# Cross-covariance attention and a squared-ReLU MLP on one core: a later second product for the first group, spread-out weight preparation, and another order of the last matmuls and stores

## Chip, cores and metric

The kernel runs on 1 core of one Trainium2 chip. The metric is the device time in microseconds of one execution, lower is better. The granted clock of the core's TensorE is given beside it where it matters.

## What is computed

```python
def _attn_ref(q, k, v, tau):                  # q, k, v: [4, 6080, 256] float32
    qn = q / (np.linalg.norm(q, axis=1, keepdims=True) + 1e-06)
    kn = k / (np.linalg.norm(k, axis=1, keepdims=True) + 1e-06)
    s = kn.transpose(0, 2, 1) @ qn / tau      # [4, 256, 256]
    s = s - s.max(-1, keepdims=True)
    a = np.exp(s)
    a /= a.sum(-1, keepdims=True) + 1e-09
    return (v @ a).astype(np.float32)
...
def _moe_ref(x, w_in, w_out, s, b):           # x: [24320, 256], w_in: [256, 2048], w_out: [2048, 256]
    h = x @ w_in
    r = np.maximum(h, 0.0)
    g = s * (r * r) + b
    return (g @ w_out).astype(np.float32)
```

The attention's output, reshaped to 24,320 rows, is the input `x` of the second function.

## The kernel before

For each of the 4 batches a 256 x 256 Gram matrix of k and q is summed over 6,080 rows, with the squares of k and q beside it. From it come the attention weights, and these are multiplied into `w_in` ("folds", lines 264 to 292), so that the MLP's first product is v times a folded 256 x 2048 weight `wa`.

**The start.** Batch 0 is done ahead of everything else: its rows come in 13 chunks (0 to 12), the last two with half as many rows per partition. For each chunk TensorE does the Gram matmuls (`mm`, line 142), and ScalarE and VectorE the squares. After some of the chunks the loop at line 398 calls `keep_busy` (line 392), matmuls whose result nobody reads. Then `finish_ops` computes the softmax and the first folds; six further folds are put into the main loop by `at_step`.

**The main loop.** The 24,320 rows of v are cut into groups of 512 rows (48 groups, 0 to 47; the last has 256). One step `s` of the loop at line 685 is one of the 16 tiles of 128 hidden features of one group, `g, m = divmod(s, 16)`. At each step the program emits, in this order:

- `mm1` (line 532): two matmuls from the transposed v and `wa` into half of an `h_ps` PSUM tile; there are two such tiles, each for two steps. The same two are used by the transposes of v by TensorE for groups 0 and 1.
- for group g - 1 some of the 112 matmuls of `seven_items` (line 670), which do the product with `w_out` in seven products instead of eight, with the sums `S1` to `S4` of g and with the weight combinations `T1`, `T2`, `T3`, `N4`. They start at tile `SHIFT` = 3 of group g.
- for the groups in `plain` (0 and 47), `plain_mm2` (line 578): the plain product with `w_out`, four matmuls a step for a whole group and two for the last group. It is `PLAG` = 5 steps behind `mm1`.
- on odd steps `relu` (line 542, ScalarE) of two steps' `h_ps`; then squares (lines 553 and 555), sums (lines 598 to 604), and what `at_step` has put on this step.

What `at_step` puts on steps includes `rowconst_sum` (lines 424 and 427, VectorE: the sum of the rows of `w_out`, in pieces `w`), `rowconst_mm` (line 431 on TensorE, line 432 on VectorE; every evacuation adds its result `rowconst`), and `combine_w` (lines 440 to 446), which makes T1, T2, T3 and N4 out of the four pieces: per piece and half-step two VectorE operations and one ScalarE copy that reads the result of one of them. `load_v`, `crossbar_v` (transposing DMAs on SP's queue), and the Gram work of the later batches are placed in the same way; Gram work of batch 1 starts at step 26. The PSUM tile of `rowconst_mm` is the one that the Gram sum of the next batch and the folds use.

`po` keeps the program's order on every engine, DMA queues included: a waiting instruction holds up all that come behind it on its engine. `store` (line 565) sends a finished group from `o_sb` to HBM on SP's queue.

Of the kernel before, what the change touches and what calls it, by code (L numbers as in the profile page):

```python
# [16 lines left out]
def kernel(  # L17
# [12 lines left out]
    nc = tc.nc  # L30
    P = 128
# [14 lines left out]
    FT = Dff // P  # L46
    TG = 512
    NG = (NT + TG - 1) // TG
# [5 lines left out]
    def po(ins):  # L54

        tc.keep_in_program_order(ins)
        return ins
# [296 lines left out]
    g0 = grams[0]  # L354
# [27 lines left out]
    NPIECE = FT // 4  # L382
# [6 lines left out]
    g0.start()  # L389
    NCH0 = len(g0.chunks)  # L390

    def keep_busy(n, w, x):

        idle_ps = h_tile("idle_ps")[:, 0, :]
        for _ in range(n):
            po(nc.tensor.matmul(idle_ps, w, x, start=True, stop=True, skip_group_check=True))

    for c in range(NCH0):
        ops = g0.norm_ops(c)
        if c >= NCH0 - 3:  # L400
            g0.add_norms()
        for j in range(g0.chunks[c][2]):
            g0.mm(c, j)
        if NCH0 - 4 <= c < NCH0 - 1:
            keep_busy(3, g0.tiles[c][1][:, 0, :P],
                      g0.tiles[c][0][:, :2, :].rearrange("p j c -> p (j c)"))
        for f in ops:
            f()
# [13 lines left out]
    def rowconst_sum(i):  # L422
        if i < NPIECE - 1:
            po(nc.vector.tensor_add(acc, w_pieces[0] if i == 0 else acc, w_pieces[i + 1]))
        else:
            n = 2 if i == NPIECE - 1 else 1
            po(nc.vector.tensor_add(acc[:, :n], acc[:, :n], acc[:, n : 2 * n]))
# [6 lines left out]
    def combine_w(i, step):  # L434
        w = w_pieces[i].rearrange("p (i h) c -> p h i c", h=2)
        B11, B12 = w[:, 0, :, :P], w[:, 0, :, P:]
        B21, B22 = w[:, 1, :, :P], w[:, 1, :, P:]
        part = ts(i, 2)
        if step == 0:
            po(nc.vector.tensor_sub(T1[:, part, :], B12, B11))  # L440
            po(nc.vector.tensor_sub(B12, B22, B12))
            po(nc.scalar.copy(out=T3[:, part, :], in_=B12))
        else:
            po(nc.vector.tensor_add(B12, B12, B11))
            po(nc.scalar.copy(out=T2[:, part, :], in_=B12))
            po(nc.vector.tensor_sub(N4[:, part, :], B21, B12))
# [4 lines left out]
    def at_step(s, f):  # L451
        side.setdefault(int(s), []).append(f)

    first_group = [b * N // TG for b in range(B)]
    for i, f in enumerate(fin[7:]):
        at_step(i // 2 * 4 + i % 2 + 1, f)
    at_step(14, lambda: po(nc.vector.tensor_scalar_mul(
        out=s_out, in0=s_bc, scalar1=1.0 / (LAM * LAM))))
    for i in range(NPIECE + 1):
        at_step(11 + i, lambda i=i: rowconst_sum(i))  # L460
    at_step(11 + NPIECE + 1, rowconst_mm)
    for i in range(NPIECE):
        for step in range(2):
            at_step(20 + i + 4 * step, lambda i=i, step=step: combine_w(i, step))
    for g in range(NG):
        if g >= 3:
            at_step(max(g - 4, 0) * FT + 2, lambda g=g: load_v(g))
# [89 lines left out]
    def evacuate(dst, src, add, n):  # L557
        if n == 1:
            add = add[:, None, :].broadcast_to((P, 2, add.shape[-1]))
        po(nc.vector.scalar_tensor_tensor(out=dst, in0=src, scalar=s_out, op0=ALU.mult,  # L560
                                          in1=add, op1=ALU.add))

    def store(g):
        t0, nj = group(g)
        po(nc.sync.dma_start(
            out=out[t0 : t0 + nj * P, :].rearrange("(p j) d -> p j d", j=nj),
            in_=o_sbs.pop(g)[:, :nj, :]))

    def plain_mm2(g, m):

        _, nj = group(g)
        for h in range((nj + 1) // 2):
            js = [j for j in (2 * h, 2 * h + 1) if j < nj]
            if m == 0:
                o_plain[g, h] = ps_o.tile([P, 2, C], FP32, tag="o_ps", name="o_ps")
            o = o_plain[g, h]
            for j in js:
                po(nc.tensor.matmul(  # L578
                    o[:, j % 2, :], g_tiles[g][:, m % 2, m // 2, ts(j, P)],
                    w_out16[:, m, :], start=(m == 0 and j == js[0]),  # L580
                    stop=(m == FT - 1 and j == js[-1]), skip_group_check=True))
            if m == FT - 1:
                if h == 0:
                    o_sbs[g] = opool.tile([P, TG // P, C], FP32, tag="o_sb", name="o_sb")
                evacuate(o_sbs[g][:, js[0] : js[-1] + 1, :], o, rowconst, 1)
                if js[-1] == nj - 1:
                    store(g)
# [18 lines left out]
    def seven_items(g):  # L606
        st = {}
        lo, hi = slice(0, P), slice(P, C)
        G = lambda h, t: lambda: g_tiles[g][:, h, :, ts(t, TG // 2)]
        W = w_out16.rearrange("p (i h) c -> p h i c", h=2)  # L610
        U = lambda: upool.tile([P, 2, P], FP32, tag="u", name="u")

        def out_sb(t, half):
            if g not in o_sbs:
                o_sbs[g] = opool.tile([P, TG // P, C], FP32, tag="o_sb", name="o_sb")
            return o_sbs[g][:, ts(t, 2), half]

        def p1():
            st["u1"] = U()
            evacuate(st["u1"], st["X"], rowconst[:, lo], 1)  # L620

        def p5():
            st["u5"] = U()
            evacuate(st["u5"], st["Z"], rowconst[:, hi], 1)

        def p6():
            st["u2"] = U()
            evacuate(st["u2"], st["X"], rowconst[:, hi], 1)

        def p2():  # L630
            evacuate(out_sb(0, lo), st["Y"], st["u1"], 2)

        def p7():
            evacuate(out_sb(1, hi), st["X"], st["u5"], 2)

        def p3():
            evacuate(out_sb(0, hi), st["Z"], st["u2"], 2)

        def p4():
            evacuate(out_sb(1, lo), st["X"], rowconst[:, lo], 1)  # L640
            store(g)

        def begin(name):
            t = ps_o.tile([P, 2, 2 * P], FP32, tag="o_ps", name="o_ps")
            halves = [t[:, h, :].rearrange("p (j c) -> p j c", j=2) for h in range(2)]
            if name == "X":
                st["X"] = halves[0]
                x_tile[0] = t
            else:
                st["Z"], st["Y"] = halves  # L650

        products = [
            ("X", G(0, 0), W[:, 0, :, lo], p1),
            ("Z", lambda: S[1], T1, p5),
            ("X", lambda: S[2], T2, p6),
            ("Y", G(1, 0), W[:, 1, :, lo], p2),
            ("X", lambda: S[3], T3, p7),
            ("Z", lambda: S[4], W[:, 1, :, hi], p3),
            ("X", G(1, 1), N4, p4),
        ]  # L660
        items = []
        for n, (name, a, w, after) in enumerate(products):
            for i in range(NP):
                for j in range(2):
                    def f(n=n, name=name, a=a, w=w, after=after, i=i, j=j):
                        first = n < 2 and i == 0 and j == 0
                        if first:
                            begin(name)
                        last = i == NP - 1 and j == 1
                        po(nc.tensor.matmul(st[name][:, j, :], a()[:, i, ts(j, P)], w[:, i, :],  # L670
                                            start=first, stop=last, skip_group_check=True))
                        if last:
                            after()
                    items.append(f)
        return items

    work = []
    NS = NG * FT
    plain = {0, NG - 1}
    PLAG = 5  # L680

    SQUARES = {3: (0, 1, nc.scalar), 5: (1, 2, nc.scalar), 8: (2, 4, nc.vector),
               12: (4, 6, nc.vector)}
# [1 line left out]
    for s in range(NS + FT):  # L685
        g, m = divmod(s, FT)
        if g < NG:
            mm1(g, m)

        if m == SHIFT and 0 < g and g - 1 not in plain:  # L690
            items = seven_items(g - 1)
            work.append((items, -(-len(items) // FT)))
        if work:
            items, n = work[0]
            for f in items[:n]:
                f()
            del items[:n]
            if not items:
                work.pop(0)
        gp, mp = divmod(s - PLAG, FT)  # L700
        if gp in plain:
            plain_mm2(gp, mp)
        if g < NG and m % 2 == 1:
            relu(g, m // 2)
            if g in plain:
                square(g, m // 2, m // 2 + 1, nc.vector)
        if g < NG and g not in plain and m in SQUARES:
            square(g, *SQUARES[m])
        if m == 0 and 0 < g and g - 1 not in plain:
            square(g - 1, 6, 8, nc.vector)  # L710
        if 0 < g and g - 1 not in plain and m in SUMS:
            sums_of(g - 1, SUMS[m])
        for f in side.pop(s, []):
            f()
# [34 lines left out]
```

## Time and profile before

| What | Value |
|---|---|
| median of 9 runs | 749.4 us (747.21 to 752.74) |
| the profiled execution's own time | 748.9 us |
| its span, first to last instruction | 747.1 us |
| mean granted TensorE clock | 0.987 |
| TensorE busy | 712.3 us (95%) |
| VectorE busy | 625.7 us (84%) |
| ScalarE busy | 538.2 us (72%) |
| TensorE, first four of 40 equal slices (18.7 us each) | 4, 7, 8 and 6 tenths busy |
| TensorE, fifth to 39th slice | 9 tenths or more |

The profile is one execution. "Busy" is a sum over instructions of an engine, and says nothing on whether they were on the path that set the end. Each line of a timeline has a start in us from the beginning of the span, a duration, engine, line of the code, operation, what it writes and reads, and in brackets how long the engine was idle before and what released it. DMA queues are called SPq (issued by SP), ACTq and POOLq.

### The profile page before, as it was taken

To read this page: it belongs to the slowest core of one execution; us is meant where nothing else is said; L and a number is where in the kernel's file an instruction comes from. 1 tells how busy PE (TensorE), PEld (TensorE's weight loads), DVE (VectorE), ACT (ScalarE), POOL (GpSimd) and SP (SyncE) were. 2 spreads that over 40 slices of the span, in tenths; PEclk is the share of its full clock that TensorE was granted. 3 is DMA by queue.
4 is the path that set the end of the run, shared out by engine and by line. 5 is a ranking of instruction groups with operands and counts; after the bars stand their busy time and mean duration, and the time that the engine had idled before them with its cause. 6 is when DMAs were issued, how large, how long until landed. Compare 5 with 4: busy or idle time off the path is not lost.

```text
span 747.1 us, 17802 instructions
## 1 busy us (share of the span) xinstructions
PE 712.3 (95%) x7600; PEld 511.2 (68%) x7600; DVE 625.7 (84%) x872; ACT 538.2 (72%) x573; POOL 83.2 (11%) x159
## 2 busy tenths in 40 slices
PE   4786999999999999999999999999999999999996
PEld 2543577776677777777668777777767777777776
DVE  4756899998888898989778898988888888888886
ACT  5454877777877777777777877877787777777772
POOL 4520321000102101000200111000000000000000
PEclk9898899999999999999999999999999999999999
DMA  9996969534645757432574647623232333321201
GB/s 236 209 254 115 173 111 149 116 72 86 147 88 101 140 129 121 97 88 69 102 140 106 133 91 131 141 65 72 81 74 61 72 97 73 91 61 44 79 29 71
DMA packets 83519, 80.60 MB, mean 108 GB/s; under 512 B 55696, under 2 KB 58576, under 8 KB 83440
## 3 DMA queue, kind: packets, MB, share of 16 engines
q0 software_dynamic: 23536, 40.51, 31.7%
q1 hardware_dynamic: 59616, 37.91, 19.0%
q8 instruction: 59, 0.97, 0.5%
q10 hardware_dynamic: 288, 1.05, 0.4%
q14 instruction: 20, 0.16, 0.1%
HBM read 81.00 MB, written 24.90 MB: 142 GB/s over the span
## 4 chain that ended last, share of the span: by engine, by line
PE 81%; DVE 6%; DMA 5%; ACT 5%; issue 2%; POOL 0%; SPq 0%; POOLq 0%; DVEq 0%; ACTq 0%
PE h_ps L532 39%; PE o_ps L670 35%; PE s_ps L142 4%; ACT r L542 2%; DMA w_out<-in_moe_w_out_dram 2%; DVE g L555 2%; DMA qk<-in_q_dram 1%; PE o_ps L578 1%; DMA raw<-in_k_dram 1%; PE wa_ps L274 1%; DMA qk<-in_k_dram 1%; ACT g L553 1%; DVE S L598 1%; DVE wa L269 1%; DVE o_sb L560 1%
## 5 line engine op out<-in xcount | busy, mean ns | idle before, releaser
L542 ACT ACTIVATE r<-h_ps 128x1024 f16<-128x1024 f32 (+1 forms) x384 | 387.7, 1013 | 170.9 <-PE h_ps L532 168.7
L532 PE MATMUL h_ps<-vT,wa 128*128 128x512 f16 (+7 forms) x1632 | 455.5, 366 | 7.4 <-ACT r L542 6.5
L670 PEld LDWEIGHTS <-S 128*128 128x128 f16 x2944 | 198.2, 98 | 85.8 <-DVE S L598 1.0
L670 PEld LDWEIGHTS <-g 128*128 128x128 f16 x2208 | 155.3, 98 | 75.4 <-issue 1.2
L555 DVE TENSOR_TENSOR g<-r 128x2048 f16<-128x2048 f16 (+2 forms) x154 | 176.7, 1148 | 25.1 <-ACT r L542 24.9
L670 PE MATMUL o_ps<-T,S 128*128 128x128 f16 x2208 | 183.7, 219 | 1.0 <-DVE S L598 0.7
L532 PEld LDWEIGHTS <-wa 128*128 128x128 f16 x1632 | 137.0, 98 | 31.9 <-issue 9.5
L670 PE MATMUL o_ps<-w_out,g 128*128 128x128 f16 x1472 | 134.7, 219 | 0.0
L560 DVE SCALAR_TENSOR_TENSOR o_sb<-o_ps,s_out,u 128x256 f32<-128x256 f32 x138 | 66.4, 481 | 57.1 <-PE o_ps L670 53.8
L553 ACT ACTIVATE g<-r 128x1024 f16<-128x1024 f16 x92 | 96.7, 1051 | 0.0
L142 PE MATMUL s_ps<-qk 128*128 128x256 f16 (+1 forms) x384 | 72.9, 292 | 14.6 <-ACT qk L133 6.8
L319 POOL DMA_DIRECT2D v<-in_v_dram x48 | 25.8, 537 | 534.6 <-DMA vT<-v 371.1
L560 DVE SCALAR_TENSOR_TENSOR u<-o_ps,s_out,rowconst 128x256 f32<-128x256 f32 x138 | 65.9, 477 | 1.4 <-PE o_ps L670 1.4
L670 PE MATMUL o_ps<-N,g 128*128 128x128 f16 x736 | 63.6, 219 | 0.9 <-ACT nrm L222 0.9
L670 PE MATMUL o_ps<-w_out,S 128*128 128x128 f16 x736 | 63.6, 219 | 0.0
L165 ACT ACTIVATE sq<-qk 128x1024 f16<-128x1024 f16 (+3 forms) x49 | 50.6, 1034 | 10.9 <-DMA qk<-in_k_dram 6.3
L600 DVE TENSOR_TENSOR S<-S,g 128x2048 f16<-128x2048 f16 x46 | 56.3, 1224 | 1.3
L604 DVE TENSOR_TENSOR S<-g,S 128x2048 f16<-128x2048 f16 x46 | 55.9, 1215 | 0.0
L602 DVE TENSOR_TENSOR S<-g 128x2048 f16<-128x2048 f16 x46 | 55.9, 1215 | 0.0
L598 DVE TENSOR_TENSOR S<-g 128x2048 f16<-128x2048 f16 x46 | 55.9, 1214 | 0.0
L142 PEld LDWEIGHTS <-qk 128*128 128x128 f16 (+1 forms) x384 | 33.9, 104 | 21.4 <-DVE qk L132 8.9
L560 DVE SCALAR_TENSOR_TENSOR o_sb<-o_ps,s_out,rowconst 128x256 f32<-128x256 f32 (+1 forms) x49 | 24.3, 498 | 13.1 <-PE o_ps L670 6.0
(67 smaller groups left out, 283.9 us busy)
## 6 DMA issues: line engine op xcount, KB each, us to landing
out_dram<-o_sb SPq DMA_DIRECT2D x47, 512.0 KB, 3.0
v<-in_v_dram POOLq DMA_DIRECT2D x47, 256.0 KB, 3.7
qk<-in_k_dram POOLq DMA_DIRECT2D x42, 256.0 KB, 6.8
qk<-in_q_dram POOLq DMA_DIRECT2D x42, 256.0 KB, 7.5
vT<-v SPq DMA_TRANSPOSE x182, 2.8
w<-in_moe_w_out_dram POOLq DMA_DIRECT2D x4, 512.0 KB, 13.7
raw<-in_q_dram ACTq DMA_DIRECT2D x2, 512.0 KB, 6.3
raw<-in_k_dram SPq DMA_DIRECT2D x2, 512.0 KB, 6.8
```

The lines of the kernel that those rows point to most:

```text
L142: po(nc.tensor.matmul(self.s_ps[:, ch, :], kc[:np_, j, ts(ch, P)], qc[:np_, j, :], start=(c == 0 and j == 0 and ch == 0), stop=(c == len(s ...
L165: po(nc.scalar.activation(out=st["sq"][:np_, 1, js, :], in_=kc[:np_, js, :], func=AF.Square))
L532: po(nc.tensor.matmul(dst, wa[:, ci, ts(m, P)], src, start=(ci == 0), stop=(ci == CH - 1), skip_group_check=True))
L542: po(nc.scalar.activation(out=r16[:, :, i % 2, :n], in_=h_tiles.pop((g, i))[:, :, :n], func=AF.Relu))
L553: po(nc.scalar.activation(out=dst, in_=src, func=AF.Square))
L555: po(nc.vector.tensor_mul(dst, src, src))
L560: po(nc.vector.scalar_tensor_tensor(out=dst, in0=src, scalar=s_out, op0=ALU.mult, in1=add, op1=ALU.add))
L598: po(nc.vector.tensor_add(S[1], A21, A22))
L600: po(nc.vector.tensor_sub(S[2], S[1], A11))
L602: po(nc.vector.tensor_sub(S[3], A11, A21))
L604: po(nc.vector.tensor_sub(S[4], A12, S[2]))
L670: po(nc.tensor.matmul(st[name][:, j, :], a()[:, i, ts(j, P)], w[:, i, :], start=first, stop=last, skip_group_check=True))
```

## The change

Five edits. The product with `w_out` of group 0 runs twelve steps behind `mm1` instead of five (group 47 stays at five). `rowconst_sum` goes from steps 11 to 15 to steps 14, 16, 18, 20 and 22, `rowconst_mm` from step 16 to 26, and `combine_w` from steps 20 to 27 (both halves of four pieces: first halves at 20 to 23, second halves at 24 to 27) to steps 24 to 31, one half a step, piece by piece. The `keep_busy` matmuls between chunks go from 3 each after chunks 9, 10 and 11 to 2 each after chunks 4 to 6, 4 each after chunks 7 to 10, and 1 after chunk 11. The matmuls of `seven_items` for group 46 are emitted eight a step instead of seven. Group 46 is stored in two halves, the first as soon as its two row blocks are done, and the store of group 47 is issued by ScalarE.

```diff
+    FILL = {-9: 2, -8: 2, -7: 2, -6: 4, -5: 4, -4: 4, -3: 4, -2: 1}
...
-        if NCH0 - 4 <= c < NCH0 - 1:
-            keep_busy(3, g0.tiles[c][1][:, 0, :P],
+        fill = FILL.get(c - NCH0, 0)
+        if fill:
+            keep_busy(fill, g0.tiles[c][1][:, 0, :P],
                       g0.tiles[c][0][:, :2, :].rearrange("p j c -> p (j c)"))
...
     for i in range(NPIECE + 1):
-        at_step(11 + i, lambda i=i: rowconst_sum(i))
-    at_step(11 + NPIECE + 1, rowconst_mm)
+        at_step(14 + 2 * i, lambda i=i: rowconst_sum(i))
+    at_step(26, rowconst_mm)
     for i in range(NPIECE):
         for step in range(2):
-            at_step(20 + i + 4 * step, lambda i=i, step=step: combine_w(i, step))
+            at_step(24 + 2 * i + step, lambda i=i, step=step: combine_w(i, step))
...
-    def store(g):
+    def store(g, j0=0, j1=None):
         t0, nj = group(g)
-        po(nc.sync.dma_start(
-            out=out[t0 : t0 + nj * P, :].rearrange("(p j) d -> p j d", j=nj),
-            in_=o_sbs.pop(g)[:, :nj, :]))
+        j1 = nj if j1 is None else j1
+        o_sb = o_sbs.pop(g) if j1 == nj else o_sbs[g]
+        po((nc.scalar if g == NG - 1 else nc.sync).dma_start(
+            out=out[t0 : t0 + nj * P, :].rearrange("(p j) d -> p j d", j=nj)[:, j0:j1, :],
+            in_=o_sb[:, j0:j1, :]))
...
         def p3():
             evacuate(out_sb(0, hi), st["Z"], st["u2"], 2)
+            if g == NG - 2:
+                store(g, 0, 2)
 
         def p4():
             evacuate(out_sb(1, lo), st["X"], rowconst[:, lo], 1)
-            store(g)
+            store(g, 2 if g == NG - 2 else 0)
...
-    PLAG = 5
+    PLAG = {0: 12, NG - 1: 5}
...
-            work.append((items, -(-len(items) // FT)))
+            work.append((items, 8 if g == NG - 1 else 7))
...
-        gp, mp = divmod(s - PLAG, FT)
-        if gp in plain:
-            plain_mm2(gp, mp)
+        for gp in plain:
+            mp = s - PLAG[gp] - gp * FT
+            if 0 <= mp < FT:
+                plain_mm2(gp, mp)
```

## The prediction, made before the changed kernel was run

> **What bounds the kernel now.** I read the page's engine rows and slices first, then the chain that ended last, then the timeline of TensorE, VectorE and ScalarE between 26 and 92 us and after 715 us, and last the table by windows.
>
> ```profile
> span 747.1 us, 17802 instructions
> ...
> PE 712.3 (95%) x7600; PEld 511.2 (68%) x7600; DVE 625.7 (84%) x872; ACT 538.2 (72%) x573; POOL 83.2 (11%) x159
> ...
> PE   4786999999999999999999999999999999999996
> ...
> PE 81%; DVE 6%; DMA 5%; ACT 5%; issue 2%; POOL 0%; SPq 0%; POOLq 0%; DVEq 0%; ACTq 0%
> ```
>
> TensorE is the bound from the fifth slice on; no edit takes a needed matmul away. What can move lies in the first four slices (75 us) and behind the last matmul. Up to 34.3 us TensorE waits for chunks of q and k: the DMA share stands at 1.04 to 1.19 in every 4 us window from 4 to 36 us. Then the stalls, from TensorE's and VectorE's timelines:
>
> ```profile
> 60.92 0.70 PE L431 MATMUL rc_ps<-acc,ones 128*128 128x256 f32 x2 [2.17 <-DVE acc L427]
> ...
> 66.60 1.46 PE L532 MATMUL h_ps<-vT,wa 128*128 128x512 f16 x6
> 70.20 1.02 PE L532 MATMUL h_ps<-vT,wa 128*128 128x512 f16 x4 [2.14 <-ACT r L542]
> 72.66 1.01 PE L532 MATMUL h_ps<-vT,wa 128*128 128x512 f16 x2 [1.44 <-ACT r L542]
> ```
> ```profile
> 66.58 1.41 DVE L560 SCALAR_TENSOR_TENSOR o_sb<-o_ps,s_out,rowconst 128x512 f32<-128x512 f32 x2 [4.45 <-PE o_ps L578]
> ```
>
> At step 16 `rowconst_mm` stops TensorE for 2.17 us, because VectorE is still adding. At step 20 VectorE stands 4.45 us before the last plain product, with the weight combinations behind it; ScalarE's copies T wait for these, the ReLUs wait behind the copies, and steps 24 and 26 wait for ReLUs. The table by windows shows the second price:
>
> ```profile
> 58.40:61.80 3.40, 1.23 (x8) 0.65 (x6) 2.61 (x6) 0.10 (x1) 0.20 (x1) 1.00 0.24 35
> 61.80:65.20 3.40, 3.40 (x14) 1.76 (x12) 0.34 (x1) 1.02 (x1) 1.40 (x3) 0.50 0.72 113
> 65.20:68.60 3.40, 2.86 (x17) 1.57 (x16) 1.98 (x4) 1.97 (x2) 0.00 (x0) 1.00 0.67 119
> 68.60:72.00 3.40, 1.02 (x4) 0.39 (x4) 2.47 (x7) 3.18 (x6) 0.00 (x0) 1.00 0.62 195
> 72.00:75.40 3.40, 2.29 (x6) 0.84 (x6) 2.69 (x6) 2.07 (x4) 0.21 (x1) 0.51 0.19 39
> 75.40:78.80 3.40, 3.18 (x10) 1.31 (x10) 3.19 (x7) 2.84 (x6) 3.40 (x7) 0.50 0.69 109
> ```
>
> Columns after the width are busy us of TensorE, its weight loads, VectorE, ScalarE, GpSimd, then clock, DMA share, GB/s. Each stretch in which TensorE works 1.0 to 1.2 of 3.4 us is followed by one or two at clock 0.50. So the stage pays twice: stalls of 2.17, 2.14, 1.44, 0.68, 0.66 and 0.33 us (7.4), and half of the slow busy time, (3.4 + 2.3 + 3.2) / 2 = 4.4 us. 11.8 in all.
>
> **What the Trainium skill says.** "TensorE: Matmul & The Clock Gate", section "What's actually happening": the clock falls to half after about one idle 3.4 us window and returns after one busy one. The trace agrees on the length (0.50 from 61.9 to 65.3 us), but a window 31% busy was enough (68.6 row), and the second fall lasts two windows. The same page, "Architectural detail", calls ScalarE and VectorE strict FIFO; the wait of ReLUs behind copies agrees. "DMA: Bandwidth & Descriptors", section "Issuing engines are not separate DMA queues": a second issuing engine saves only sequencer time. The trace before has no store on ACTq to compare.
>
> **The main edit and the weight combinations, laid out step by step.** I go through program order with durations of the rows: `mm1` 0.435 a step (pairs start 0.43 apart), plain product 0.44, fold 0.43, ReLU 1.02 (the next ScalarE work 0.92 after), T copy 0.40, square 0.69 for group 0 and 1.23 later, evacuation 0.75, combination 0.42, Gram pair 0.22, sums of rows 1.22. I start at the end of step 5's `mm1` (45.0 us), the same in both.
>
> - Steps 6 to 14. Without the plain product TensorE doesn't wait for `w_out` (0.36), but has nothing to put into its waits: at steps 6 and 10 a fold waits for ScalarE's evacuation behind a ReLU (0.85 and 0.84), at 8 and 12 `mm1` waits for VectorE's (0.37 each), at 14 for a ReLU (0.68; the transposes of v took the other buffer). Step 14 starts at 54.65, before 55.98: 1.3 earlier, but owing seven plain products, 7 x 0.44 = 3.1 us. Judged alone, this costs.
> - Steps 14 to 25. 0.87 us a step, TensorE without a gap (ReLU and square together stay below two steps' 1.74). `rowconst_sum` runs beside it: VectorE has 0.69 + 1.22 = 1.9 us in the worst two steps, done by 61.0. Stall 2.17 gone. Step 24 starts at 63.35.
> - Step 24. Square (lines 4 to 7 of the group's tiles) needs the ReLU ending at 64.26, then 1.23, two combinations 0.8: ScalarE's copy at 66.3, having waited 2.05.
> - Step 26. **The wait that is added**: `rowconst_mm` (0.70) ends at 66.65; the Gram matmul behind it needs the same PSUM tile, thus line 432, which stands behind step 25's combinations: 67.65. TensorE loses 1.0; step 27's `mm1` and the last plain product stand behind it.
> - Step 27. Plain product done at 68.74; two evacuations to 70.05; combination, copy at 70.45 (waited 0.9, and 0.4 at 26). Step 28: square to 72.07, combinations, copy at 72.8 (waited 2.0). The ReLU of step 29 runs 73.1 to 74.1, those of 31 and 33 end at 76.6 and 77.9.
> - TensorE does steps 28 to 31 to 70.93, then stands to 74.15 for the ReLU of 29 (step 32), and to 76.65 for that of 31 (step 34).
> - Step 35, first of the seven products: 77.9 at full clock, before 81.80. The 3.2 us stall should bring slow windows, as in the table; steps 32 to 36 are then longer. One window costs 0.7, a second would cost 1.7 more. I take one: **3.2 us gained**. Bounds 1.0 (two windows, waits somewhat longer) to 6.5 (the stall vanishes: VectorE's 27.0 us of work in the 44 us of the table leave room).
>
> Check by sums: before 11.8 + 0.36; after waits 0.85 + 0.37 + 0.84 + 0.37 + 0.68 + 1.0 + 3.2 = 7.3, second wait 0.3, slow clock 0.7: 12.2 - 8.3 = 3.9. I keep the lower, 3.2.
>
> What moves along: SP's store of group 0 goes from step 20 to 27. It held the transposes of group 3 behind it for 14.8 us (SP's waits); now they pass it. Nobody waits for that store; GpSimd's load of batch 1's third chunk waits for the first combined piece (12.0 us, to 75.19) and goes at 68.0, wanted at step 44. Group 0's g and PSUM tiles are held to step 27, wanted again at step 35. All zero; if a cover failed, the price is a 2.8 us transpose landing.
>
> **Fillers.** 23 instead of 9 matmuls, 0.216 us each (three in 0.81 less the overlap). A chunk takes 1.03 us, 1.86 at half clock, and comes every 2.5 us. With two fillers 1.46, with four 1.9: hidden in the wait for DMA. They should lift the 0.50 clock of 21 to 27.7 us, where nothing waits for TensorE. After chunk 11 two fewer lie ahead of the last chunk, which comes at 34.3 anyway: 0 to 0.1 gained. If the clock stays low a four-filler chunk takes 3.4 us, TensorE falls 0.9 behind per chunk until a busy window passes, and 0.5 may remain. I take 0; -0.1 to +0.5.
>
> **Eight a step.** The same matmuls, so the last one ends at 742.2 as before. 13 x 0.055 = 0.7 us more stands ahead of the last `mm1` (740.06 instead of 739.34); ReLU and square end at 741.2, wanted at 741.8. S4, now behind one more evacuation, ends at 737.6, wanted at 738.1. Zero; if these 0.5 us are missing, up to 0.5 lost.
>
> **Stores.** The end:
>
> ```profile
> 742.11 1.25 SPq L565 DMA_DIRECT2D out_dram<-o_sb  x2
> 742.25 0.75 DVE L560 SCALAR_TENSOR_TENSOR o_sb<-o_ps,s_out,rowconst 128x512 f32<-128x512 f32 x1 [0.17 <-PE o_ps L578]
> ```
>
> Both stores (768 KB) moved from 743 to 745, at 406 and 348 GB/s, so group 47's 256 KB stood behind group 46's 512. Now the first half of 46 leaves at about 740.2, the second at 741.6, and 256 KB at 0.65 us are out of the way: 0.4 gained, between 0 and 0.7. ScalarE has no work after its last ReLU; its queue's issue cost isn't shown, by SP's row 0.33.
>
> **Sum.** 3.2 + 0 + 0 + 0.4 = 3.6. The profiled execution had 748.9, the median is 749.4; I take the gain from the median: **745.8**. About 0.3% (2.2 us) is what a measurement of this kernel can tell from no change.
>
> **Rivals.**
> - *The stage eases further* (0.12). TensorE's stall at step 32 shrinks because copies wait less than laid out; 742.9. For it: ScalarE's work between 64.3 and 76.9 is only 7.3 of 12.6 us. Against: order fixes its waits.
> - *Wait for wait* (0.20). The 3.2 us stall brings two slow windows (1.7 more), fillers leave 0.4: 3.6 - 2.1 = 1.5, **747.9**. For it: 72.0 to 78.8 us before. Against: TensorE has nothing owed at the second window.
> - *Slower* (0.08). ScalarE's eight copies, one a step, each behind VectorE: laid out they wait 5.35 us. If every copy waits 2.05 as the first does, that is 16.4, 11 more, against 3.6 gained: 757. It decides from 5.8 more on (11.2 in all). Against: three copies in a row (29 to 31) find VectorE ahead.
> - *No effect of the lag* (in the second case): had TensorE idled for `w_out`, the lag would gain; it idled 0.36.
>
> Likeliest case 0.60, 743.8 to 747.1. Nearly all of it and of the first rival is faster, 0.69; same 0.22, slower 0.09. The range goes from 743.0 to 748.8: it holds the likeliest and most of the first two rivals.
>
> **What would show it.** Right: no wait at line 431; step 14's `mm1` near 54.7 us with waits of 0.8 before folds; a wait near 1 us at step 26 for line 432; a wait of 2 to 4 us for ReLU before step 32; the first line 670 matmul near 78.4; last store's landing near 2.0. Wrong: a slow clock between 48 and 66 us, or line 670 starting after 80.

## Result: 745.16 us against 749.57, and the profile after

| What | before | after |
|---|---|---|
| median | 749.57 us (31 runs, 747.21 to 752.74) | 745.16 us (10 runs, 744.62 to 746.86) |
| ratio, with its 95% interval | | 0.9944 (0.9933 to 0.9955) |
| profiled execution, its span | 748.9, 747.1 us | 744.89, 743.0 us |
| first `mm1` starts | 40.07 us | 40.11 us |
| first of the seven products (group 1) starts | 81.80 us | 78.28 us |
| last evacuation starts | 742.25 us | 738.58 us |
| from there to the end of the span | 4.85 us | 4.42 us |

The change makes the kernel 0.56% faster. The ten runs after lie in two groups, six at 744.6 to 745.3 us (mean clock 0.996 to 0.998) and four at 746.1 to 746.9 (0.995), and the profiled one is of the first. The two profiles place the 4.1 us of the spans: 3.6 are won between the first `mm1` and the first of the seven products, 0.4 behind the last evacuation, and the 660 us between agree to 0.15, so what was priced at zero there shows no cost.

The page after, engines and slices:

```profile
span 743.0 us, 17832 instructions
...
PE 710.7 (96%) x7614; PEld 511.0 (69%) x7614; DVE 626.0 (84%) x872; ACT 538.3 (72%) x573; POOL 83.5 (11%) x159
...
PE   4777999999999999999999999999999999999997
...
PE 82%; DVE 6%; ACT 5%; DMA 4%; issue 2%; POOL 0%; DVEq 0%; ACTq 0%; POOLq 0%
```

Fourteen more matmuls (the fillers) and yet 1.6 us less TensorE time, because less of it ran at half clock. The digits changed in the second to fourth slice and in the last, nowhere between. Of the chain, DMA went from 5% to 4%: the `w_out` load of before (14.10 us) is out of it.

TensorE's timeline after, the places where a stall stood before or was forecast (start, duration, engine, line; in brackets the idle time before and its releaser):

```profile
52.16 0.39 PE L535 MATMUL h_ps<-vT,wa 128*128 128x512 f16 x1 [0.20 <-DVE wa L269]
...
65.53 0.60 PE L434 MATMUL rc_ps<-acc,ones 128*128 128x256 f32 x2
67.82 0.38 PE L142 MATMUL s_ps<-qk 128*128 128x256 f16 x2 [1.69 <-DVE rowconst L435]
...
74.43 0.89 PE L535 MATMUL h_ps<-vT,wa 128*128 128x512 f16 x2 [3.20 <-ACT r L545]
...
76.89 1.55 PE L535 MATMUL h_ps<-vT,wa 128*128 128x512 f16 x4 [0.30 <-ACT r L545]
78.28 0.55 PE L677 MATMUL o_ps<-w_out,g 128*128 128x128 f16 x7
```

From 52.16 to 65.53 TensorE has no wait to show; the matmul of the row sums (line 434 now) runs as soon as its turn comes. Two stalls are new: 1.69 us before the first Gram matmul at step 26, and 3.20 us at step 32. ScalarE's timeline says what the second waits for:

```profile
66.05 0.40 ACT L445 CAST T<-w 128x256 f16<-128x256 f32 x1 [2.09 <-DVE w L444]
66.36 1.02 ACT L545 ACTIVATE r<-h_ps 128x1024 f16<-128x1024 f32 x1
...
68.59 0.40 ACT L445 CAST T<-w 128x256 f16<-128x256 f32 x1 [0.92 <-DVE w L444]
...
70.66 0.41 ACT L448 CAST T<-w 128x256 f16<-128x256 f32 x1 [0.74 <-DVE w L447]
73.05 0.40 ACT L445 CAST T<-w 128x256 f16<-128x256 f32 x1 [1.98 <-DVE w L444]
73.36 1.02 ACT L545 ACTIVATE r<-h_ps 128x1024 f16<-128x1024 f32 x1
```

Four of the eight copies T wait, 5.73 us in sum, each for a combination that VectorE reaches late: behind a square (the first and the fourth copy) or behind other combinations, `rowconst` and the evacuations (the two between). The fourth, at 73.05, matters most. VectorE comes to its combination only after a square:

```profile
71.00 1.22 DVE L558 TENSOR_TENSOR g<-r 128x2048 f16<-128x2048 f16 x1
...
72.59 0.42 DVE L444 TENSOR_TENSOR w<-w 128x256 f32<-128x256 f32 x1
```

The ReLU of step 29 stands behind this copy in ScalarE's order, although its matmuls had been done since about 70.2 us. It starts at 73.36, ends at 74.38 and lets step 32 go at 74.43.

The table by windows after (width, busy us of TensorE, weight loads, VectorE, ScalarE, GpSimd, then clock, DMA share, GB/s):

```profile
58.40:61.80 3.40, 3.40 (x26) 2.29 (x24) 2.57 (x4) 2.69 (x4) 0.00 (x0) 1.00 1.36 125
61.80:65.20 3.40, 3.40 (x25) 2.27 (x24) 1.21 (x2) 2.16 (x3) 1.59 (x3) 1.00 0.51 84
65.20:68.60 3.40, 1.72 (x13) 1.10 (x11) 2.78 (x8) 1.63 (x4) 0.64 (x2) 1.00 0.98 173
68.60:72.00 3.40, 2.63 (x17) 1.44 (x15) 3.08 (x5) 1.72 (x3) 1.34 (x3) 1.00 0.83 127
72.00:75.40 3.40, 0.97 (x4) 0.47 (x4) 2.59 (x7) 2.35 (x4) 1.11 (x3) 0.88 0.91 160
75.40:78.80 3.40, 3.10 (x17) 1.39 (x16) 2.81 (x5) 2.98 (x6) 2.52 (x6) 0.62 1.15 240
```

Before, three stretches here were at about half clock; now it is one, across the last two rows: means of 0.88 and 0.62 are 0.8 and 2.6 us at half clock, 3.4 in all.

The end, lines of VectorE's and the queues' timeline:

```profile
736.45 1.88 SPq L570 DMA_DIRECT2D out_dram<-o_sb  x2
...
738.58 0.75 DVE L563 SCALAR_TENSOR_TENSOR o_sb<-o_ps,s_out,rowconst 128x512 f32<-128x512 f32 x1 [0.61 <-PE o_ps L583]
739.36 0.35 ACTq L570 DMA_DIRECT2D out_dram<-o_sb  x1
```

Group 46's two halves leave from 736.45 on; group 47's store leaves by ScalarE's queue, right after its evacuation.

### The profile page after: what moved, and what is told of

Same layout as the page of the kernel before. It is cut to its first block, busy times and chain, and to the rows that moved or that the text cites. A ratio compares the mean times of both kernels' runs of the same rounds, so it can differ in the third digit from the quotient of the medians.

```text
span 743.0 us, 17832 instructions
## 1 busy us (share of the span) xinstructions
PE 710.7 (96%) x7614; PEld 511.0 (69%) x7614; DVE 626.0 (84%) x872; ACT 538.3 (72%) x573; POOL 83.5 (11%) x159
## 4 chain that ended last, share of the span: by engine, by line
PE 82%; DVE 6%; ACT 5%; DMA 4%; issue 2%; POOL 0%; DVEq 0%; ACTq 0%; POOLq 0%
PE h_ps L535 40%; PE o_ps L677 35%; PE s_ps L142 4%; ACT r L545 2%; DVE g L558 2%; DMA qk<-in_q_dram 2%; DMA qk<-in_k_dram 1%; PE wa_ps L274 1%; DMA w_in<-in_moe_w_in_dram 1%; ACT g L556 1%; DVE wa L269 1%; PE o_ps L583 1%; DVE S L603 1%; ACT wa L267 1%; DVE o_sb L563 1%
## 5 line engine op out<-in xcount | busy, mean ns | idle before, releaser
L142 PE MATMUL s_ps<-qk 128*128 128x256 f16 (+1 forms) x384 | 71.1, 286 | 14.9 <-ACT qk L133 7.1
L162 DVE TENSOR_TENSOR sq<-qk 128x1024 f16<-128x1024 f16 (+3 forms) x49 | 32.9, 672 | 2.5 <-DMA qk<-in_q_dram 2.5
```

Of the source, the lines that this page charges most:

```text
L142: po(nc.tensor.matmul(self.s_ps[:, ch, :], kc[:np_, j, ts(ch, P)], qc[:np_, j, :], start=(c == 0 and j == 0 and ch == 0), stop=(c == len(s ...
```

## The experiments

My theory: each engine keeps the program's order, so a wait of one instruction is passed to all behind it, and the time is set by how the row sums, the combinations, the copies and the plain product of group 0 stand to each other between steps 14 and 35. The rivals were other answers to "which edit gains": the lag, the spread combinations, or the fillers. "First product" is always the start of the first of the seven products; before it stands at 81.80, after at 78.28.

**e1: the combinations on their old steps.**

```diff
-            at_step(24 + 2 * i + step, lambda i=i, step=step: combine_w(i, step))
+            at_step(20 + i + 4 * step, lambda i=i, step=step: combine_w(i, step))
```

> The changed kernel with the weight combinations put back on steps 20 to 27 (first halves at 20 to 23, second at 24 to 27); everything else as changed. My theory (engines in program order, the stall of step 32 comes from ScalarE's copies waiting behind VectorE): the first halves now fall into VectorE's idle 2.9 us at 61 to 64 us, no copies are left on steps 28 to 31, so the ReLU of step 29 ends near 72.8 instead of 74.4 and the wait before step 32 shrinks from 3.20 to about 0.9 us; the wait for rowconst at step 26 grows from 1.7 to about 2; first product of the seven at 75.5 to 76 instead of 78.3. About 2.7 us faster than the changed kernel (1.5 to 4): ratio to before near 0.991. Rival (the spreading of the combinations is where the gain comes from): 2 us or more slower than the changed kernel, ratio 0.997 or above, with the stalls of before at steps 24 and 26.

742.17 us, ratio 0.9897 (0.9881 to 0.9914): 3.0 us faster than the changed kernel. TensorE's timeline, and below it two lines of ScalarE's:

```profile
68.47 0.38 PE L142 MATMUL s_ps<-qk 128*128 128x256 f16 x2 [1.78 <-DVE rowconst L435]
...
72.69 0.59 PE L535 MATMUL h_ps<-vT,wa 128*128 128x512 f16 x2 [0.81 <-ACT r L545]
...
74.55 1.02 PE L535 MATMUL h_ps<-vT,wa 128*128 128x512 f16 x4 [0.61 <-ACT r L545]
75.41 0.55 PE L677 MATMUL o_ps<-w_out,g 128*128 128x128 f16 x7
```
```profile
71.31 0.41 ACT L448 CAST T<-w 128x256 f16<-128x256 f32 x1 [0.97 <-DVE w L447]
71.62 1.02 ACT L545 ACTIVATE r<-h_ps 128x1024 f16<-128x1024 f32 x1
```

The stall of 3.20 became 0.81, and no window from 17 us on is slow. With the plain product out of the way at step 20, VectorE is free there: the changed kernel shows it idle for 2.92 us before the square at 63.99. The same eight copies now wait 2.92 us in sum instead of 5.73, and the ReLU of step 29 starts at 71.62 instead of 73.36. Spreading the combinations, one of the five edits, is a loss of 3 us inside the change; the rival is out.

**e2: the row sums on their old steps.**

```diff
-        at_step(14 + 2 * i, lambda i=i: rowconst_sum(i))
-    at_step(26, rowconst_mm)
+        at_step(11 + i, lambda i=i: rowconst_sum(i))
+    at_step(11 + NPIECE + 1, rowconst_mm)
```

> The changed kernel with the row sums back on steps 11 to 15 and their matmul on step 16. My theory: TensorE stops at step 16 from 57.3 to about 60.0 us for VectorE's sums (2.7 us, before 2.17), the wait at step 26 (1.69) goes; the ReLU of step 23 is some 3 us later and ScalarE's chain of copies follows it, so about 2 us slower than the changed kernel, ratio 0.997. Rival (it is hidden by the waits that follow, as the 3.2 us stall at step 32 only shrinks): within 0.5 us of the changed kernel, ratio 0.9944.

749.76 us, ratio 0.9995 (0.9985 to 1.0004): the whole gain is gone, 4.6 us against the 2 expected. The stall is as forecast in kind, and of the size of before:

```profile
59.87 0.70 PE L434 MATMUL rc_ps<-acc,ones 128*128 128x256 f32 x2 [2.21 <-DVE acc L430]
...
77.17 1.01 PE L535 MATMUL h_ps<-vT,wa 128*128 128x512 f16 x2 [2.80 <-ACT r L545]
...
81.30 0.95 PE L677 MATMUL o_ps<-w_out,g 128*128 128x128 f16 x7
```

The later stall shrank little, to 2.80, because ScalarE's chain follows the ReLU of step 23: that one starts 3.6 us later than in the changed kernel (66.50 against 62.94), the ReLU of step 29 still 2.7 later. And seven matmuls took 0.95 us instead of 0.55: half clock reaches into the products here. With the combinations spread, the gain needs the moved row sums.

**e3: the old fillers.**

```diff
-    FILL = {-9: 2, -8: 2, -7: 2, -6: 4, -5: 4, -4: 4, -3: 4, -2: 1}
+    FILL = {-4: 3, -3: 3, -2: 3}
```

> The changed kernel with the old filler matmuls (3 each after chunks 9, 10, 11). My theory: nothing waits for TensorE there; the clock of 0.50 between 21 and 28 us comes back and the first mm1 still starts at 40.1 us, time within 0.3 us of the changed kernel, ratio 0.9944. Rival (the warm clock is a gain): first mm1 0.5 to 1.2 us later, ratio 0.995 to 0.996.

747.52 us (744.84 to 748.5), ratio 0.9958 (0.9941 to 0.9976). This interval overlaps that of the changed kernel (0.9933 to 0.9955), but the eight runs lie in two groups, three at 744.8 to 745.1 and five at 747.4 to 748.5, and these five are slower than every run of the changed kernel (highest 746.86). The profiled one is of the second group. The windows of it (columns as above):

```profile
24.30:27.70 3.40, 2.73 (x14) 1.74 (x13) 2.86 (x6) 1.30 (x2) 1.18 (x4) 0.50 1.12 209
27.70:31.10 3.40, 2.78 (x12) 1.50 (x11) 2.21 (x4) 1.87 (x2) 1.98 (x3) 0.50 1.13 205
31.10:34.50 3.40, 3.40 (x51) 2.54 (x50) 2.15 (x4) 1.26 (x2) 2.82 (x4) 0.50 1.24 207
34.50:37.90 3.40, 3.40 (x34) 2.02 (x33) 0.42 (x1) 0.00 (x0) 2.01 (x3) 0.74 1.10 214
```

The half clock that the kernel before had from 20.9 to 27.7 us reaches to 36 here. Chunks, column sums and the old fillers then take twice as long where TensorE does have a schedule to keep: it is busy without a gap from 31.1 on, and the first `mm1` starts at 42.98 instead of 40.11. Both theories missed: mine (within 0.3 us) holds in the first group only, and the rival's 0.5 to 1.2 us is too small for the second.

**e4: the end as before.**

```diff
-            work.append((items, 8 if g == NG - 1 else 7))
+            work.append((items, 7))
...
-            if g == NG - 2:
-                store(g, 0, 2)
...
-            store(g, 2 if g == NG - 2 else 0)
+            store(g)
...
-        po((nc.scalar if g == NG - 1 else nc.sync).dma_start(
+        po(nc.sync.dma_start(
```

> The changed kernel with the end as before: seven matmuls a step for group 46, its store in one piece, group 47's store on SP's queue. My theory: the last evacuation ends at the same distance from the first product, the end of the span is 4.1 us after it instead of 3.67: 0.4 us slower than the changed kernel, ratio 0.995. Rival (the stores ran side by side anyway): no difference in the distance from the last evacuation to the end, ratio 0.9944.

745.95 us, ratio 0.9948 (0.9933 to 0.9963). The interval overlaps that of the changed kernel, so the times don't decide. The traces do: from the start of the last evacuation (739.43) to the end of the span (744.3) it is 4.87 us, as in the kernel before (4.85), and 4.42 after. The same holds over all twelve traces: 4.78 to 4.90 in the six with the old end (before, e4, e5, e6, e9, e10), 4.42 to 4.50 in the six with the new one. The 0.4 us belongs to the end. Which part of it does this, the store of group 46 in halves or the last store on ScalarE's queue, was not tried apart.

**e5: the lag alone, on the kernel before.**

```diff
-    PLAG = 5
+    PLAG = {0: 12, NG - 1: 5}
```

> The kernel before with one edit: the plain product of group 0 twelve steps behind. My theory now (e1 and e2 in hand): the row sums still stop TensorE for 2.2 us at step 16, but the old places of the combinations are good once the plain product no longer blocks VectorE at step 20; first product of the seven at 76.5 to 78 us where the start of the main loop is at 40.1, so nearly all of the change's gain by itself: ratio 0.993 to 0.996, with executions some 3 us longer where the clock falls late in the chunks (old fillers). Rival (laid out in the prediction for steps 6 to 14: the lag alone costs): ratio 1.000 to 1.004.

746.54 us, ratio 0.9971 (0.9960 to 0.9982). It gains 3.0 us by the medians and 2.2 by the ratio, so the step-by-step reading that it costs (up to step 14) didn't carry to the end. It is less than expected (0.993 to 0.996): the first product comes 39.1 us after the first `mm1` (41.52 to 80.65), not 36.4 to 37.9, since the stall at step 16 is 2.20 us and half clock follows it from 62.8 to 66.2 us.

**e6: the spread combinations alone, on the kernel before.** The edit is the reverse of e1's.

> The kernel before with one edit: the combinations on steps 24 to 31, one half a step. My theory: the stall before step 24 goes (no copies before the ReLU of step 21), but eight copies then each stand between ReLUs with VectorE behind, and the ReLUs of 29 and 31 end near 79 and 81.5; first product near 82.9, so 0 to 3 us slower than before, ratio 1.000 to 1.004. Rival (the spreading is a gain): ratio 0.996 to 0.998.

751.66 us, ratio 1.003 (1.0018 to 1.0042): 2 us slower. The stall before step 24 shrank to 0.25 us as expected (before 2.14), and TensorE waits 2.17 us for a ReLU at step 28. The edit costs with either lag, which agrees with e1. The profiled execution starts `mm1` at 41.44 us, so its first product (83.95) isn't comparable with that of before.

**e7: the lag back at 5, everything else as changed.** The row sums stand on steps 11 to 15 and their matmul on 19, since group 0's evacuation at step 20 adds their result.

```diff
-    PLAG = {0: 12, NG - 1: 5}
+    PLAG = {0: 5, NG - 1: 5}
...
-        at_step(14 + 2 * i, lambda i=i: rowconst_sum(i))
-    at_step(26, rowconst_mm)
+        at_step(11 + i, lambda i=i: rowconst_sum(i))
+    at_step(19, rowconst_mm)
```

> The changed kernel with the lag of group 0 back at 5 (the row sums on steps 11 to 15 and their matmul on 19, as the first plain evacuation on step 20 needs them); combinations, fillers and end as changed. My theory: the row sums' stall is gone either way, and ScalarE's chain of copies decides; it starts some 1.9 us later and waits 1.2 less, first product near 79.1 instead of 78.3: ratio near 0.9955. Rival (the lag is what gains, as it fills TensorE's waits of steps 16 to 27): 3 us slower than the changed kernel, ratio 0.998 or more.

746.46 us, ratio 0.9960 (0.9949 to 0.9970); first product at 79.09, as expected to the tenth. With the row sums' matmul three steps later than before the stall at it is gone (none at 61.92), so the lag, with the later places that it allows the row sums, is worth 1.3 us among the other edits; the two intervals just overlap (0.9949 to 0.9970 against 0.9933 to 0.9955). A part of it is the wait for `w_out` before the first plain product, 1.14 us here and none with the lag of 12. The rival's 3 us are out, though e5 shows 3.0 where nothing else is changed: the lag and the moved row sums overlap.

**e8: combinations on their old steps, row sums' matmul on 23.** On top of e1:

```diff
-    at_step(26, rowconst_mm)
+    at_step(23, rowconst_mm)
```

> As e1 (combinations on their old steps), and the matmul of the row sums on step 23 instead of 26, where VectorE stands idle. My theory: the wait of 1.78 us for rowconst at step 26 goes, VectorE's chain stays (square, three combinations, two evacuations), so ReLU 29 ends near 71.8 instead of 72.6 and TensorE waits 2.3 us before step 32 instead of 0.8: first product at 74.6, 0.8 us faster than e1, ratio 0.9887. Rival (that longer wait brings a slow window): no better than e1, 742 to 743 us, clock 0.50 in a window after 72 us.

741.41 us, ratio 0.9904 (0.9874 to 0.9933), the fastest version by its times: its four runs (741.25 to 741.88) lie below all five of e1 (742.07 to 742.29), while the intervals of the ratios overlap. First product at 74.65 (expected 74.6), 0.8 us earlier than in e1. The wait at step 26 is gone; TensorE waits 0.84, 0.34, 0.87 and 0.62 us for ReLUs instead of one wait of 2.3, and no window from 17.5 us on is slow. The single long wait was wrong, the sum (2.7) near.

**e9: the new fillers alone, on the kernel before.** The edit is the reverse of e3's, on the kernel before.

> The kernel before with one edit, the new fillers. My theory after e3 (the 0.50 clock after thin windows falls late in some executions and then stretches chunks 9 to 12 and the fillers there; the new fillers keep the clock up from chunk 4 on): the first mm1 stands at 40.0 us in every execution, the lowest times stay at 747.3, the median falls by 1 to 2 us: ratio 0.9975 to 0.9985. Rival (as predicted, nothing waits for TensorE there and e3's late start was chance): ratio 0.9995 or above, spread as before.

748.23 us, ratio 0.9986 (0.9977 to 0.9995). No run is above 750.1, where 4 of the 27 runs of before beside it are above 751. The profiled execution has clock 1.00 in each window from 17.5 to 68 us and the first `mm1` at 40.07. So the fillers gain some 1.4 us in the median and next to nothing in the best case (747.24 against 747.53). The profiles of all versions agree with this: the eight with the new fillers start `mm1` between 39.92 and 40.11 us, the four with the old ones at 40.07, 41.44, 41.52 and 42.98.

**e10: the lag and the new fillers, on the kernel before.** The edits of e5 and e9 together.

> The kernel before with two edits: the lag of 12 and the new fillers; row sums, combinations and end as before. My theory (parts add where each keeps its own stall away): first product near 78 us with the row sums' 2.2 us stall at step 16 left, and 1 to 1.5 us below e5: 745.3, ratio 0.9945, as good as the whole change. Rival (the moved row sums and combinations are needed for the gain): no better than e5, 746.5, ratio 0.997.

746.76 us, ratio 0.9961 (0.9946 to 0.9976), no better than e5: my expectation fell. The first `mm1` stands at 40.06, but the stall at step 16 (2.21 us) is followed by half clock from 60.2 to 63.6 us, and the first product comes at 79.59. e1 differs from this version in the moved row sums and in the end only, and is 4.6 us faster; the end is worth 0.4, so beside the lag the moved row sums are worth some 4 us. e5 has executions of 745.2 us with the same stall. They may be those in which no half clock follows it, as in e9 and e2 (last section): without it this version would take some 745.1 us, an estimate from 3.4 us of busy TensorE at half clock. It is not shown, as each version has one profile.

## Why the prediction was right, and where it wasn't

The forecast was 745.8 us within 743.0 to 748.8, faster; measured 745.16.

- **The layout of steps held.** Step 14 was put at 54.65 us and stands at 54.25; the plain product's last matmul at step 27 was put to end at 68.74 and is evacuated from 68.89; the stall at step 32 was put at 3.2 us and is 3.20; the first product at 78.4 (78.6 by the sum of its parts) and stands at 78.28. Following each engine's order with durations from the rows was enough. That the stall agrees to the digit is in part luck: the waits at steps 8, 12 and 14, put at 0.37, 0.37 and 0.68, were 0.20, 0.20 and none, and step 26 lost 0.7 us more than laid out.
- **The added wait at step 26 was undersized**: 1.0 forecast, 1.69 measured. I missed a wait of VectorE for ScalarE, 0.47 us: the second half of a combination overwrites `w`, which the copy still reads.

VectorE's timeline of the changed kernel:

```profile
66.48 0.42 DVE L447 TENSOR_TENSOR w<-w 128x256 f32<-128x256 f32 x1 [0.47 <-ACT T L445]
66.94 0.42 DVE L449 TENSOR_TENSOR N<-w 128x256 f16<-128x256 f32 x1
67.29 0.48 DVE L435 TENSOR_SCALAR rowconst<-rc_ps,b_bc 128x256 f32<-128x256 f32 x1
```

It cost nothing in the end, since the stall at step 32 waits for ScalarE's chain, not for TensorE's.

- **One slow window after that stall** was assumed at a cost of 0.7 us, and 3.4 us at half clock were seen. Most of them ran while TensorE would have waited for the ReLU of step 31 anyway; what counts is some 0.5 us, since the first product starts 1.39 us after step 34 (76.89 to 78.28), and 0.86 after it in e1 (74.55 to 75.41) at full clock. The Trainium skill's "TensorE: Matmul & The Clock Gate", section "HAM oscillation — how this bites in real kernels", says that a wait longer than the window lets the clock fall. Here waits shorter than 3.4 us were enough: 2.17 us in the kernel before, 2.21 in e10. But the same wait at the same step, 2.17 us in e9 and 2.21 in e2, was followed by full clock; the last section shows what differs.
- **Stores**: 0.4 us forecast, 0.43 measured, e4 agrees. **Eight a step**: no new stall of TensorE at the end (0.69 us for S1 before and after), as forecast; it wasn't tried apart from the stores.
- **The fillers were mis-sized**: 0 forecast (-0.1 to +0.5), about 1.4 us (e9) to 2.4 us (e3) measured in the medians. The failing step: "hidden in the wait for DMA" was read from one execution, in which the slow stretch ended at 27.7 us. In others it reaches the last chunks (to 32.1 us in e5, 32.5 in e6, 36.3 in e3), where nothing hides it. So a part of the median's gain doesn't show in the two profiles, which both start `mm1` at 40.1. That the sum came so near (3.6 forecast, 4.4 between the medians) is therefore partly luck; between the lowest runs the gain is 2.6 us (747.21 to 744.62).
- **The combinations' move was not seen as a loss.** The prediction priced its waits (5.35 us; 5.73 measured) but not the other places that the lag makes free; e1 shows that leaving them where they were is worth 3.0 us. The rival "the stage eases further", with 742.9, is about what e1 gets.
- **Which edit gains** was not separated: 3.2 us were given to the lag and the combinations together. In the changed kernel the moved row sums are worth 4.6 us (e2) and the lag 1.3 (e7), and the spread combinations cost 3.0 (e1). These overlap and don't add up to the whole. Moved row sums with nothing else changed were not tried.
- **The other rivals.** "Slower" is out: the copies wait 5.73 us, not 16.4. "Wait for wait", two windows at half clock after the 3.20 us stall, doesn't hold in the profiled execution, which shows one. e4, with the same stall, shows two (73.1 to 79.9 us, mean clock 0.994). The four slower runs of the changed kernel (0.995) lie 1.8 us above the six others in the median, near the 1.7 that the prediction gave a second window; that they are such executions is not shown. "No effect of the lag" rested on 0.36 us of waiting for `w_out`; with the new fillers and the lag of 5 this wait is 1.06 (e9) and 1.14 us (e7).
- **"Judged alone, this costs"**, said of the lag at steps 6 to 14, is right for these steps (TensorE reaches step 14 earlier by 1.7 us, 55.98 to 54.25, owing 3.1 us of plain products) but e5 is 3.0 us faster in the whole: the owed work falls into later waits, and those for ReLUs before the first product shrink from 4.6 us in sum (before) to 2.5 (e5).

## What to carry to other kernels

Where engines keep the program's order, place a chain over several engines where the engine that feeds it stands idle, not evenly: the same eight copies waited 5.73 us when spread one a step among the ReLUs, and 2.92 when four of them stood at steps where VectorE was idle. When an edit clears a place in the order, look again at all that was put elsewhere because of it. And a clock that follows activity makes one profile a sample: an edit that gains nothing in it can still be worth a microsecond in the median.

## What the runs showed of the hardware that was not expected

- In each trace the changes of the granted clock lie whole multiples of about 3.41 us apart: at 20.8, 27.7, 61.8, 65.2, 72.0 and 78.9 us in the kernel before. When the time is cut at these points, one number of a piece tells what follows. In the ten traces that show a change, from 15 us to the first product, each of the 17 falls from 1.00 to 0.50 came after a piece with TensorE busy between 0.21 and 1.52 us, and no piece at full clock with 1.70 us or more was followed by a fall. At 1.52 both were seen (e6 fell, the changed kernel at 20.0 us didn't). Where these points lie in the program differs between the profiled executions, so the same stall can fall into one piece or be divided between two. The stall of 2.17 us at step 16, in the kernel before and then in e9 (columns as above):

```profile
58.42:61.83 3.41, 1.24 (x7) 0.63 (x6) 2.62 (x6) 0.08 (x1) 0.23 (x1) 1.00 0.24 34
61.83:65.24 3.41, 3.41 (x14) 1.76 (x12) 0.31 (x1) 1.02 (x1) 1.36 (x3) 0.50 0.73 115
```
```profile
57.25:60.66 3.41, 2.20 (x17) 1.34 (x14) 3.41 (x7) 1.02 (x1) 0.00 (x0) 1.00 0.89 121
60.66:64.07 3.41, 2.45 (x15) 1.67 (x16) 1.39 (x3) 1.02 (x1) 1.59 (x3) 1.00 0.20 18
64.07:67.49 3.42, 3.02 (x18) 1.66 (x17) 1.85 (x4) 1.97 (x2) 0.00 (x0) 1.00 1.03 180
```

- With the old fillers the main loop starts at different times, and it follows the end of the slow stretch before it: 40.07, 41.52, 41.44 and 42.98 us where that ended at 27.7 (before), 32.1 (e5), 32.5 (e6) and 36.3 (e3). e3's two groups are 3.1 us apart in their medians (744.92 and 748.05). That they are an early and a late start is read from one profile of the late group, and not shown for every run.
